# A fused attention, SiLU block and top-1 expert kernel: two weight slices change homes, the last routing goes behind the first expert tiles, and tile facts, staging and padding are re-timed

## Chip, cores and metric

The kernel runs on one core of a Trainium2 chip. The metric is the device time of one execution in microseconds; the kernel before has a median of 801.7 us over three runs (801.68 to 804.72).

Engines are named as in the profile: PE is TensorE, PEld its weight loads, ACT is ScalarE, DVE is VectorE, POOL is GpSimd, SP is SyncE, which here issues nearly all DMAs in one queue.

## What is computed

Three stages, each on the output of the one before; cut from the reference:

```
# 1. gated linear attention: 4 batches x 8 heads, 768 steps, head size 48
state = alpha[:, :, t, :, None] * state + einsum('bhd,bhe->bhde', k[:, :, t], v[:, :, t])
y[:, :, t] = einsum('bhd,bhde->bhe', q[:, :, t], state)
# 2. dense block on x = y as (3072 tokens, 384): 384 -> 2048 -> 384
h = x @ w_in;  g = h * (1.0 / (1.0 + exp(-h)));  x = g @ w_out
# 3. one expert of 8 for each token: 384 -> 1024 -> 384
logits = normalized(x) @ normalized(expert_emb).T / tau
expert_idx = argmax(logits, axis=1);  probs = softmax(logits)
out[mask] = gate_w[mask, None] * (relu(x[mask] @ w1[e]) @ w2[e])
```

## The kernel before

Numbers are kept as pairs of 16-bit halves (names with h and l, high and low part), and each product is three matmuls: high x high, high x low, low x high.

**Attention** works on 24 chunks of 128 tokens (names `S`, `yp`, `KT`, `ys`); its steps are mixed into the dense stage and end about 460 us into the span.

**The dense block** runs in 8 blocks of 384 tokens, 0 to 7, with 16 pieces of 128 hidden units (`f`). For each piece `mm1` forms `hp` in PSUM (9 matmuls, L1059), ACT makes `g` by SiLU and its high half (L1066, L1067), DVE the low half (L1068), and `mm2` adds 9 matmuls (L1082) into the three sums `o0` to `o2`. Pieces take turns on three buffers: two lie in the tile of `w2l` slice 7, the third is `g3` (shown as `g`). The input `x` of a block lies in three turns in tiles of w2's last two slices, which are only filled when the blocks no longer need them.

**Routing.** `route` takes the sums of 128 tokens after a block: square norm on ACT (L1105), logits, arg max, a rank by a small matmul (L1120, L1121), all on DVE, and scatters the row to its expert's region of the buffer `xs_d` in memory (L1149, POOL). The last block's three tiles are routed among the first expert tiles.

**Weights of the experts** (`w1`: 3 slices, `w2`: 8 slices, in 384 or 512 KB loads) are loaded by SP into a staging area `work` of 3072 words a partition, then converted to halves by ACT and DVE (L650, L651; for some L548, L551 on ACT and L552 on POOL). `begin_w` starts loads, `convert_w` converts the oldest, once per piece of blocks 6 and 7. In block 6 two loads are in flight, in block 7 three.

**Experts.** `early` (block 7) and `tile_list` (after the last routing) make a list of 28 tiles: 24 of one expert, 4 of two halves. For each tile `prep_load` loads the transposed rows `xT` and the facts `mt` (token number, scale, logits) on SP; `expert1` multiplies by `w1` in two halves of 9 matmuls (L1394) into one of two PSUM buffers, ACT takes the relu (L1400), DVE the low half (L1401); `send` transposes by DMA on SP (L1369) into `hT` (buffers `g`, `hb`, `work`); `expert2` multiplies by `w2` in 24 matmuls (L1422); ACT scales the result into `ob` (L1430, one buffer) and POOL scatters it to the output (L1433). `prep_fac` turns the logits of a tile into its gate weight: an Exp on ACT (L1359), which needs another function table than SiLU, and three small DVE operations. Before, it is called two tiles ahead, and its place on ACT is left to the scheduler. `write_pads` (L1313) copies 128 dummy rows behind each expert's last row, all eight at once on POOL after `tile_list`.

**Order.** A scheduler that builds the program places instructions on each in-order engine from its own estimate of times; where the code calls `behind(ins, other)`, an instruction is kept behind another one on the same engine. `lead["a"]` and `lead["g"]` are the latest SiLU or relu pieces on ACT and DVE, `lead["o"]` (new) the latest output scatter.

## Time and profile before

| quantity | value |
|---|---|
| median of three runs | 801.7 us |
| profiled execution, own time | 807.86 us |
| its span, first to last instruction | 806.3 us |
| busy share of the span: PE, DVE, ACT, POOL | 94%, 62%, 52%, 28% |
| mean granted PE clock | 0.981 |
| DMA queue of SP, share of 16 engines | 50.0% |

The profiled execution took 6.2 us more than the median run. The span splits into attention with blocks 0 to 5 (to about 464 us), block 6 (to 514), block 7 (to about 570), the first expert tiles, and the other tiles to about 800 us.

### The profile page before, as it was taken

What the parts mean: (1) busy time and instruction counts of PE and PEld (TensorE: products, weight loads), DVE (VectorE), ACT (ScalarE), POOL (GpSimd) and SP (SyncE); (2) the same over time, 40 slices, a digit from 0 to 9 for tenths busy, and PEclk for the clock granted to TensorE, in tenths of its full rate; (3) what the DMA queues carried; (4) which work ended last, traced back from release to release, by engine and by line L of the source; (5) the groups of instructions that cost most, each with busy time, mean ns of one, the idle gap of its engine ahead of it and who ended that gap; (6) DMA issues with size and microseconds to landing.
All of it is one profiled execution on the core that took longest, in us unless ns stands there. A gap on an engine that the chain in (4) does not pass through costs nothing. (4 is left out here: it accounts for less than half of the span.)

```text
span 806.3 us, 16490 instructions
## 1 busy us (share of the span) xinstructions
PE 756.6 (94%) x5554; PEld 472.5 (59%) x5554; DVE 498.0 (62%) x1446; ACT 418.5 (52%) x933; POOL 221.8 (28%) x322
## 2 busy tenths in 40 slices
PE   7888999999988999999999998979799999999995
PEld 4755787676655666656666654545344455555553
DVE  6599866787677977978868586665743222222221
ACT  3454655565655866857657685656632222222221
POOL 3301113554443453544232130220233011010101
PEclk9898999999999999999999999999999999999999
DMA  9599323444356445635521455255687656676562
GB/s 195 133 285 278 58 56 60 93 87 82 86 120 109 97 111 125 129 96 113 108 78 41 100 178 165 84 143 160 178 161 171 125 118 114 119 127 109 121 102 44
DMA packets 241099, 97.93 MB, mean 121 GB/s; under 512 B 222041, under 2 KB 230398, under 8 KB 240880
## 3 DMA queue, kind: packets, MB, share of 16 engines
q1 hardware_dynamic: 237424, 85.58, 50.0%
q0 software_dynamic: 3584, 11.18, 4.1%
q8 instruction: 51, 0.84, 0.5%
q14 instruction: 40, 0.33, 0.1%
HBM read 58.39 MB, written 12.16 MB: 88 GB/s over the span
## 5 line engine op out<-in xcount | busy, mean ns | idle before, releaser
L1059 PE MATMUL hp<-w2h,wi_h 128*128 128x384 f16 x576 | 145.2, 330 | 9.6 <-ACT w2l L1066 3.4
L1082 PE MATMUL o<-wo_h,w2l 128*128 128x392 f16 x528 | 146.8, 331 | 2.5 <-ACT w2l L1067 2.0
L1059 PEld LDWEIGHTS <-wi_h 128*128 128x128 f16 x768 | 74.8, 99 | 58.1 <-issue 10.6
L1082 PEld LDWEIGHTS <-w2l 128*128 128x128 f16 x792 | 75.5, 98 | 52.8 <-ACT w2l L1067 3.1
L1394 PE MATMUL hp<-w1h,xT 128*128 (+1 forms) x384 | 101.0, 382 | 4.4 <-DVE work L1401 4.3
L1401 DVE SCALAR_TENSOR_TENSOR work<-hp,work 128x512 f16<-128x512 f32 x56 | 38.5, 690 | 96.6 <-ACT work L1400 96.4
L1059 PE MATMUL hp<-w2h,wi_l 128*128 128x384 f16 x288 | 94.6, 331 | 0.0
L1082 PE MATMUL o<-wo_l,w2l 128*128 128x392 f16 x264 | 87.2, 330 | 0.0
L1394 PEld LDWEIGHTS <-xT 128*128 128x128 f16 (+1 forms) x576 | 50.4, 101 | 61.5 <-issue 7.9
L1433 POOL DMA_INDIRECT out_dram<-ob,mt x28 | 27.5, 981 | 168.4 <-ACT ob L1430 166.7
L1082 PE MATMUL o<-wo_h,g 128*128 128x392 f16 x240 | 65.8, 329 | 1.9 <-ACT g L1067 1.6
L1394 PE MATMUL hp<-w1l,xT 128*128 (+1 forms) x192 | 64.2, 382 | 0.0
L1400 ACT ACTIVATE work<-hp 128x512 f16<-128x512 f32 x56 | 33.2, 595 | 57.8 <-PE hp L1394 53.9
L1068 DVE SCALAR_TENSOR_TENSOR w2l<-w2l 128x384 f16<-128x384 f32 x88 | 50.0, 572 | 21.1 <-ACT w2l L1067 20.6
L1066 ACT ACTIVATE w2l<-hp 128x384 f32<-128x384 f32 x88 | 42.5, 484 | 32.2 <-PE hp L1059 28.7
L1059 PEld LDWEIGHTS <-wi_l 128*128 128x128 f16 x384 | 38.2, 99 | 23.7 <-issue 1.5
L1082 PEld LDWEIGHTS <-g 128*128 128x128 f16 x360 | 34.2, 98 | 25.6 <-ACT g L1067 2.3
L1059 PE MATMUL hp<-w2l,wi_h 128*128 128x384 f16 x192 | 48.7, 330 | 0.0
L1067 ACT ACTIVATE w2l<-w2l 128x384 f16<-128x384 f32 x88 | 45.4, 522 | 4.4 <-PE o L1082 2.8
L1422 PEld LDWEIGHTS <-work 128*128 128x128 f16 (+1 forms) x384 | 33.5, 101 | 22.7 <-issue 0.4
L825 POOL TENSOR_SCALAR_AFFINE_SELECT S<-S 128x512 f32<-128x512 f32 x48 | 31.4, 677 | 55.0 <-ACT S L824 54.8
L1422 PE MATMUL po<-w2h,work 128*128 (+1 forms) x256 | 43.8, 326 | 0.0
(283 smaller groups left out, 1542.1 us busy)
## 6 DMA issues: line engine op xcount, KB each, us to landing
work<-in_moe_w_dram SPq DMA_DIRECT2D x24, 512.0 KB
work<-in_moe_w_dram SPq DMA_DIRECT2D x30, 384.0 KB
w1h<-in_moe_w_in_dram SPq DMA_DIRECT2D x6, 768.0 KB
nat_a<-in_alpha_dram SPq DMA_DIRECT2D x23, 192.0 KB
nat_k<-in_k_dram SPq DMA_DIRECT2D x23, 192.0 KB
nat_q<-in_q_dram SPq DMA_DIRECT2D x23, 192.0 KB
nat_v<-in_v_dram SPq DMA_DIRECT2D x23, 192.0 KB
w1h<-in_moe_w_out_dram SPq DMA_DIRECT2D x5, 768.0 KB
```

What stands on the lines that cost most here:

```text
L825: nc.gpsimd.affine_select(out=s, in_=s, pattern=[[0, NPAIR], [1, 128]], compare_op=ALU.is_ge, fill=0.0, base=0, channel_multiplier=-1,)
L1059: ins = nc.tensor.matmul(out=hp, lhsT=wi[a][f // 2][:, c, (f % 2) * 128:(f % 2 + 1) * 128], rhs=x[:, c, :], start=(n == 0), stop=(n == 3 * ...
L1066: nc.scalar.activation(out=g, in_=hp, func=ACTF.Silu, scale=1.0 / (SX * SWI))
L1067: lead["a"] = nc.scalar.activation(out=gh, in_=g, func=ACTF.Copy, scale=SG)
L1068: lead["g"] = nc.vector.scalar_tensor_tensor(out=gl, in0=g, scalar=SG, in1=gh, op0=ALU.mult, op1=ALU.subtract)
L1082: nc.tensor.matmul(out=acc[t], lhsT=a[:, ts], rhs=wo[w][f // 2][:, f % 2, :], start=(f == 0 and n == 0), stop=(f == KF - 1 and n == 2),)
L1394: nc.tensor.matmul(out=hp[ts], lhsT=xT[:, a, ts], rhs=w1s[w][c][:, e if isinstance(e, int) else bass.ds(e, 1), fs], start=(n == 0), stop=( ...
L1400: lead["a"] = nc.scalar.activation(out=hs[:, 0], in_=hp, func=ACTF.Relu)
L1401: lead["g"] = nc.vector.scalar_tensor_tensor(out=hs[:, 1], in0=hp, scalar=0.0, in1=hs[:, 0], op0=ALU.max, op1=ALU.subtract)
L1422: nc.tensor.matmul(out=po[ts], lhsT=hT[c // 4][:, at + ts.start:at + ts.stop], rhs=w2s[w][c][:, e if isinstance(e, int) else bass.ds(e, 1) ...
L1433: nc.gpsimd.indirect_dma_start(out=out[:, :], out_offset=bass.IndirectOffsetOnAxis(ap=d["row"], axis=0), in_=ob, in_offset=None, bounds_ch ...
```

## The change

Seven edits, none of which adds or removes a matmul, a conversion, a load or a scatter:

1. Of w2's last slices, `uni` now holds `h6`, `l6`, `l5`, `l7`; the tiles of `h5` and `h7` open at pieces 13 and 15 of block 7, when memory of the dense weights comes free. Slice 5 is thus converted before the end of block 7.
2. `place` gives each load any free words of `work`, in place of fixed slots; `begin_w` allows up to four loads in flight for all but the first slices of w1 (three are asked for in blocks 6 and 7, where block 6 had two). The routing copies of blocks 5 and 6 move out of `work`.
3. The last routing is kept behind the relu of the tiles ahead of it, and its first row uses another buffer.
4. `prep_fac` is called for a tile just before its own `expert2`, behind the newest relu.
5. The list of `early` uses a buffer of its own, not `g3`.
6. `write_pads` copies two experts' pads per tile, in the turns of tiles 2 to 5, behind the output scatter ahead of them.
7. The order of the first expert tiles is written anew: tile 0's and tile 1's `expert1` come as a whole, with slice 7's conversions between.

```diff
-        for c in (KE - 2, KE - 1):
-            for s in "hl":
-                w2s[s][c] = wu.tile([128, E, DM], FP16, name=f"w2{s}{c}")
-                uni.append(w2s[s][c].rearrange("p e d -> p (e d)"))
+        for s, c in (("h", KE - 2), ("l", KE - 2), ("l", KE - 3), ("l", KE - 1)):
+            w2s[s][c] = wu.tile([128, E, DM], FP16, name=f"w2{s}{c}")
+            uni.append(w2s[s][c].rearrange("p e d -> p (e d)"))
...
+        held, newest = [], [0]
+
+        def place(n, room=3072):
+
+            for k in range(0, room, 256):
+                at = (newest[0] + k) % room
+                if at + n <= room and all(at >= b or at + n <= a for a, b in held):
+                    newest[0] = at + n
+                    held.append((at, at + n))
+                    return at
...
             def begin():
-                st = work[:, F * (e % 2):F * (e % 2 + 1)]
+                at = place(F, 2048 if c < 2 else 3072)
+                st = work[:, at:at + F]
                 ins = nc.sync.dma_start(out=st, in_=w1[e, c * 128:(c + 1) * 128, :])
...
-        def weight2(c, e, slot, pooled=False):
+        def weight2(c, e, slot=None, pooled=False):
             def begin():
-                st = slot.rearrange("p (e d) -> p e d", e=2)
+                at = place(2 * DM) if slot is None else None
+                words = work[:, at:at + 2 * DM] if slot is None else slot
+                st = words.rearrange("p (e d) -> p e d", e=2)
                 nc.sync.dma_start(out=st, in_=w2[e:e + 2, c * 128:(c + 1) * 128, :].rearrange("e p d -> p e d"))
...
             sc = 1.0 / (SG * SWO)
-            row = m2.tile([128, ROW], FP32, name="row", **(dict(tag="sq", bufs=1) if last and n != 1 else dict(tag="row", bufs=3)))
...
-                x2 = work[:, 2048 + n * DM:2048 + (n + 1) * DM] if n < 2 else m2.tile(
-                    [128, ROW], FP32, tag="sq", name="x2", bufs=1)[:, 0:DM]
+                if n == 2:
+                    x2 = m2.tile([128, ROW], FP32, tag="sq", name="x2", bufs=1)[:, 0:DM]
+                elif j + 3 < NB:
+                    x2 = work[:, 2048 + n * DM:2048 + (n + 1) * DM]
+                else:
+                    w, at = (uni[n], 6 * DM) if j + 2 == NB else (uni[1], (4 + 2 * n) * DM)
+                    x2 = w[:, at:at + 2 * DM].bitcast(FP32)
                 unit = 1.0
                 nc.scalar.activation(out=x2, in_=acc[:, 0:DM], func=ACTF.Copy, scale=sc, accum_out=fin)
-            nc.scalar.activation(out=row[:, 0:DM], in_=x2, func=ACTF.Square, scale=unit, accum_out=ss)
+            first = [nc.scalar.activation(out=row[:, 0:DM], in_=x2, func=ACTF.Square, scale=unit, accum_out=ss)]
...
-            )
+            ))
             nc.gpsimd.tensor_copy(out=meta[:, 0:1].bitcast(I32), in_=tok[:, i:i + 1])
...
-            nc.vector.tensor_reduce(out=rm, in_=x2, axis=AXX, op=ALU.max, apply_absolute_value=True)
+            first.append(nc.vector.tensor_reduce(out=rm, in_=x2, axis=AXX, op=ALU.max, apply_absolute_value=True))
+            if last:
+                for ins, order in zip(first, (lead["a"], lead["g"], lead["g"])):
+                    behind(ins, order)
...
-                weight2(c, e, work[:, 512 * (e % 4):512 * (e % 4) + 2 * DM]) + (1,) for c in range(2) for e in range(0, E, 2)
+                weight2(c, e) + (1,) for c in range(2) for e in range(0, E, 2)
             )
 
...
-                if c == KE - 1 and e < 4:
-                    st = uni[2 + i][:, 4 * DM:].bitcast(FP32)
-                else:
-                    if c == KE - 1:
-                        i = 5 - i
-                    st = work[:, 2 * DM * i:2 * DM * (i + 1)]
+                st = None
+                if c == KE - 1:
+                    i = 5 - e // 2
+                    st = work[:, 2 * DM * i:2 * DM * (i + 1)] if e > 2 else (
+                        g3 if e else uni[3][:, 4 * DM:]).bitcast(FP32)
                 todo.append(weight2(c, e, st, (c, e) in POOLW2) + (2,))
 
-        def open_w2(c):
+        def open_w2(c, parts="hl"):
             pool = wst.enter_context(tc.tile_pool(name=f"w2{c}", bufs=1, side="left", **rel))
-            for s in "hl":
+            for s in parts:
                 w2s[s][c] = pool.tile([128, E, DM], FP16, name=f"w2{s}{c}")
 
         def begin_w(k):
-            while todo and len(late) < min(k, 3 if todo[0][2] == 2 else 2):
+            while todo and len(late) < min(k, 2 if todo[0][2] == 0 and todo[0][1] < 2 else 4):
                 begin, c, kind = todo.pop(0)
                 late.append((begin(), c, kind))
...
             return tl, tcum
 
-        def listing(tl, tcum, base, n, rows, experts):
+        def listing(tl, tcum, base, n, rows, experts, gt):
...
-            gt = g3[:, 1024:].bitcast(FP32)
             G = gt[:, 0:E * n].rearrange("p (j e) -> p j e", e=E)
...
+            gt = m2.tile([128, ROW], FP32, tag="sq", name="gt", bufs=1)
+            listing(tl, tcum, base, KEARLY, idx0, ei0, gt)
             nc.vector.tensor_sub(out=es, in0=tl, in1=tcum)
...
-            listing(tl, tcum, base, NLIST, idx[:, 0:NLIST], ei)
+            listing(tl, tcum, base, NLIST, idx[:, 0:NLIST], ei, g3[:, 1024:].bitcast(FP32))
...
-        def write_pads():
-            for e in range(E):
+        def write_pads(experts):
+            for e in experts:
                 r = nc.values_load(
                     ends[0:1, e:e + 1], engines=[mybir.EngineType.Pool], min_val=0, max_val=DUMMY - 128,
                     skip_runtime_bounds_check_because="an expert has at most NT rows and CAP is NT + 128",
                 )
...
-        def prep_fac(j):
+        def prep_fac(j, order=None):
             d = tl_[j]
             meta = d.pop("m")
             s = m2.tile([128, 2], FP32, tag="s", name="s", bufs=4)
             sm, fac = s[:, 0:1], s[:, 1:2]
             ex = m2.tile([128, E], FP32, tag="ex", name="ex")
-            nc.scalar.activation(out=ex, in_=meta[:, 2:2 + E], func=ACTF.Exp, accum_out=sm)
+            ins = nc.scalar.activation(out=ex, in_=meta[:, 2:2 + E], func=ACTF.Exp, accum_out=sm)
+            if order is not None:
+                behind(ins, order)
...
-            nc.gpsimd.indirect_dma_start(
+            lead["o"] = nc.gpsimd.indirect_dma_start(
...
                     convert_w(last)
+                    if last and f >= KF - 4:
+                        begin_w(3)
+                        convert_w(last)
                 if j > 1 and (f % 4 == 2 or done[0] >= NCH):
-                    begin_w(1 if done[0] < NCH else 2 if j + 1 < NB else 3)
+                    begin_w(1 if done[0] < NCH else 3)
                 mm2(j, f, g, acc)
                 g = nxt
                 if last:
                     if f % 2:
                         fpool[f // 2].close()
-                    if f % 4 == 3:
+                    if f % 4 == 3 and f + 1 < KF:
                         open_w2(2 + f // 4)
+                    elif f == KF - 3:
+                        open_w2(KE - 3, "h")
+                    elif f == KF - 1:
+                        open_w2(KE - 1, "h")
...
-        while todo and todo[0][1] == 5:
-            late.append((todo.pop(0)[0](), 5, 2))
-        for _ in range(2):
-            late.append((todo.pop(0)[0](), KE - 1, 2))
+        begin_w(4)
+        while late[0][1] == KE - 3:
+            convert_w()
+            begin_w(4)
+        expert1(0, 0, True)
         convert_w()
         convert_w()
-        expert1(0, 0)
-        convert_w()
-        convert_w()
-        for _ in range(2):
-            late.append((todo.pop(0)[0](), KE - 1, 2))
+        send(0, 0)
         expert1(0, 1)
         convert_w()
         convert_w()
-        expert1(1, 0, True)
-        convert_w()
-        convert_w()
-        send(1, 0)
+        expert1(1, 0)
         expert1(1, 1)
         assert not todo and not late
-        prep_fac(0)
-        prep_fac(1)
...
         expert2(1, 0)
+        prep_fac(0, lead["a"])
         expert2(0, 1)
         send(2, 0)
         send(2, 1)
         prep_load(3)
         prep_load(4)
-        prep_fac(2)
-        prep_fac(3)
         expert1(3, 0, True)
         expert1(3, 1, True)
+        prep_fac(1, lead["a"])
         expert2(1, 1)
         send(3, 0)
         send(3, 1)
         tile_list()
-        write_pads()
         order = [*range(SFULL), *range(NFULL, NFULL + SPAIR)]
         for n in range(2, len(order)):
             j = order[n]
+            if n < 6:
+                write_pads(range(2 * n - 4, 2 * n - 2))
             if n + 3 < len(order):
                 prep_load(order[n + 3])
-            if n + 2 < len(order):
-                prep_fac(order[n + 2])
             if 2 < n and n + 1 < len(order):
                 expert1(order[n + 1], 0)
...
+            prep_fac(j, lead["a"])
             expert2(j)
 
```

The build's order shows the first differences on PE, ACT and DVE at the end of block 5; on SP a load moves ahead of one transpose shortly before. Line numbers of the change are 16 to 25 higher.

First place: ACT in block 7, at pieces 5 to 9. `ex,s<-mt` is the Exp of `prep_fac`, L650 a conversion of w2, L1066 and L1067 the SiLU pieces. Before:

```order
L1067 ACTIVATE g_179<-g_179 128x384
L1066 ACTIVATE g_179<-hp 128x384
L1359 ACT_TABLE_LOAD
L1359 ACTIVATE ex,s<-mt 128x8
L1067 ACTIVATE w2l_178<-w2l_178 128x384
L650 ACTIVATE w2h_6959<-work 128x768
L1359 ACTIVATE ex,s<-mt 128x8
L1067 ACTIVATE w2l_178<-w2l_178 128x384
L650 ACTIVATE w2h_6959<-work 128x768 x2
L1067 ACTIVATE g_179<-g_179 128x384
L650 ACTIVATE w2h_6959<-work 128x768
L1359 ACTIVATE ex,s<-mt 128x8 x2
```

Now, over pieces 5 to 9 (L1082 and L1083 are the SiLU pieces, L649 the conversion):

```order
L1082 ACTIVATE g_179<-hp 128x384
L1083 ACTIVATE g_179<-g_179 128x384
L649 ACTIVATE w2h_6960<-work 128x768
L1082 ACTIVATE w2l_178<-hp 128x384
L1083 ACTIVATE w2l_178<-w2l_178 128x384
L649 ACTIVATE w2h_6960<-work 128x768
L1082 ACTIVATE w2l_178<-hp 128x384
L1083 ACTIVATE w2l_178<-w2l_178 128x384
L649 ACTIVATE w2h_6960<-work 128x768
L1082 ACTIVATE g_179<-hp 128x384
L1083 ACTIVATE g_179<-g_179 128x384
L649 ACTIVATE w2h_6960<-work 128x768
```

The four Exps and both table loads have left this place; each piece is followed by one conversion.

Second place: ACT where block 7 ends. L1105 is the first step of the last routing, L1400 the relu of an expert tile. Before:

```order
L551 ACTIVATE w2h_7173<-work 128x768
L1105 ACTIVATE row,nx<-o_6790 128x384
L650 ACTIVATE w2h_7269<-work 128x768 x2
L1105 ACTIVATE row,nx<-o_6791 128x384
L1400 ACTIVATE work<-hp_7285 128x512
L650 ACTIVATE w2h_7269<-work 128x768 x2
L1400 ACTIVATE work<-hp_7304 128x512
L650 ACTIVATE w2h_177<-w2h_177 128x768
L650 ACTIVATE w2h_177<-w2l_178 128x768
L1135 ACTIVATE row<-o_6790,nx 128x384
L1400 ACTIVATE work<-hp_7324 128x512
L650 ACTIVATE w2h_177<-work 128x768 x2
```

Now (L1126 routing, L1425 relu, L649 conversion; `w2h_7238` is slice 5, `w2h_7286` slice 7):

```order
L1083 ACTIVATE w2l_178<-w2l_178 128x384
L649 ACTIVATE w2h_7238<-work 128x768 x4
L1425 ACTIVATE work<-hp_7295 128x512
L649 ACTIVATE w2h_7286<-w2l_178 128x768
L649 ACTIVATE w2h_7286<-g_179 128x768
L1425 ACTIVATE work<-hp_7312 128x512
L649 ACTIVATE w2h_7286<-work 128x768 x2
L1425 ACTIVATE work<-hp_7332 128x512
L1425 ACTIVATE work<-hp_7345 128x512
L1126 ACTIVATE row,nx<-o_6791 128x384
L1126 ACTIVATE row,nx<-o_6792 128x384
```

The routing steps moved from ahead of the first relu to behind the fourth, and four conversions of slice 5, which stood behind the routing, stand ahead of everything.

Third place: POOL after the last routing. L1313 is a pad, L1309 the register load that it needs, L1433 an output scatter. Before:

```order
L1433 DMA out_dram<-ob,mt 3072x384
L1309 TENSOR_LOAD ends
L1313 ISA
L1313 DMA xs_d<-xs_d 16x3152
L1433 DMA out_dram<-ob,mt 3072x384
L1309 TENSOR_LOAD ends
L1313 ISA
L1313 DMA xs_d<-xs_d 16x3152
L1309 TENSOR_LOAD ends
L1313 ISA
```

Now (L1335 pad, L1331 register load, L1458 output scatter):

```order
L1458 DMA out_dram<-ob,mt 3072x384
L1331 TENSOR_LOAD ends
L1335 ISA
L1335 DMA xs_d<-xs_d 16x3152
L1331 TENSOR_LOAD ends
L1335 ISA
L1335 DMA xs_d<-xs_d 16x3152
L1458 DMA out_dram<-ob,mt 3072x384
L1331 TENSOR_LOAD ends
L1335 ISA
L1335 DMA xs_d<-xs_d 16x3152
L1331 TENSOR_LOAD ends
```

Eight pads in a row behind two scatters have become pairs with a scatter between them.

## Rows read from the trace of the kernel before

**Rows 1.** Windows: start:end, length, busy us (x instructions) PE, PEld, DVE, ACT, POOL, PEclk, DMA share, GB/s.

```profile
464.00:514.00 50.00, 47.92 (x295) 27.81 (x294) 32.16 (x110) 31.24 (x61) 7.54 (x12) 1.00 0.50 154
514.00:570.00 56.00, 49.51 (x298) 27.97 (x297) 35.42 (x129) 38.18 (x78) 12.77 (x14) 1.00 0.53 156
570.00:602.00 32.00, 26.56 (x140) 13.40 (x139) 21.28 (x93) 13.76 (x27) 8.33 (x12) 0.95 0.73 150
602.00:640.00 38.00, 35.37 (x185) 17.85 (x183) 11.31 (x42) 11.72 (x34) 10.16 (x14) 1.00 0.68 151
640.00:800.00 160.00, 156.88 (x1017) 85.02 (x1014) 37.51 (x98) 42.39 (x117) 20.45 (x21) 1.00 0.60 110
```

**Rows 2.** Waits of PE, 464 to 800 us: releaser, us in total, times, longest.

```profile
PE hp L1394 <- DVE work L1401: 4.3, 2, 4.1
PE hp L1059 <- ACT w2l L1066: 3.4, 3, 1.7
...
PE o L1082 <- ACT w2l L1067: 2.0, 3, 0.8
PE o L1082 <- ACT g L1067: 1.6, 1, 1.6
PE hp L1059 <- ACT g L1066: 1.5, 1, 1.5
```

**Rows 3.** Timeline of ACT, blocks 6 and 7: start, us, instruction [idle before <- releaser].

```profile
486.58 0.84 ACT L650 ACTIVATE w2h<-work 128x768 f16<-128x768 f32 x1 [2.06 <-DMA work<-in_moe_w_dram]
488.82 0.84 ACT L650 ACTIVATE w2h<-work 128x768 f16<-128x768 f32 x1 [1.40 <-DMA work<-in_moe_w_dram]
...
531.37 0.52 ACT L1067 ACTIVATE g<-g 128x384 f16<-128x384 f32 x1 [2.73 <-DVE g L1266]
...
534.87 1.28 ACT L1359 ACT_TABLE_LOAD   x1
538.59 0.21 ACT L1359 ACTIVATE ex<-mt 128x8 f32<-128x8 f32 x1 [2.44 <-DMA mt<-xs_d]
...
547.09 1.28 ACT L1066 ACT_TABLE_LOAD   x1
548.39 0.49 ACT L1066 ACTIVATE w2l<-hp 128x384 f32<-128x384 f32 x1
```

**Rows 4.** Timeline of ACT where block 7 ends.

```profile
570.00 1.56 ACT L650 ACTIVATE w2h<-work 128x768 f16<-128x768 f32 x2
...
572.19 0.60 ACT L1400 ACTIVATE work<-hp 128x512 f16<-128x512 f32 x1 [0.16 <-DVE w2l L651]
```

**Rows 5.** Timelines of DVE (first two rows) and PE, the same stretch.

```profile
572.41 0.93 DVE L651 SCALAR_TENSOR_TENSOR w2l<-work,w2h 128x768 f16<-128x768 f32 x1
574.07 0.68 DVE L1401 SCALAR_TENSOR_TENSOR work<-hp,work 128x512 f16<-128x512 f32 x1
...
574.80 1.01 PE L1394 MATMUL hp<-w1h,xT 128*128 x2 [4.07 <-DVE work L1401]
578.04 0.81 PE L1422 MATMUL po<-w2h,g 128*128 x4
...
580.05 0.59 PE L1394 MATMUL hp<-w1h,xT 128*128 x2
...
581.99 0.49 PE L1422 MATMUL po<-w2h,hb 128*128 x2
```

**Rows 6.** Timelines of SP's queue and PE in the tile loop: the second half's transpose, and its first use.

```profile
630.26 1.31 SPq L1369 DMA_TRANSPOSE hb<-work  x1
634.08 0.81 PE L1422 MATMUL po<-w2h,hb 128*128 x4 [1.20 <-DMA hb<-work]
...
691.73 1.25 SPq L1369 DMA_TRANSPOSE hb<-work  x1
696.53 0.81 PE L1422 MATMUL po<-w2h,hb 128*128 x4
```

**Rows 7.** DMA issues, 560 to 640 us: issue, KB each, median us to landing.

```profile
xs_d<-xs_d POOLq DMA_DIRECT2D x8, 197.0 KB, 2.9
```

More of the change, by code (lines that the diff above doesn't have):

```diff
@@ L667, in convert @@
                 def convert():
+                    held.pop(0)
                     split_after(st, SW1, w1s["h"][c][:, e, :], w1s["l"][c][:, e, :])
@@ L1092, in route @@
             sc = 1.0 / (SG * SWO)
-            row = m2.tile([128, ROW], FP32, name="row", **(dict(tag="sq", bufs=1) if last and n != 1 else dict(tag="row", bufs=3)))
+            row = m2.tile([128, ROW], FP32, name="row", **(dict(tag="sq", bufs=1) if last and n == 0 else dict(tag="row", bufs=3)))
             meta, x16 = row[:, DM:], row[:, 0:DM].bitcast(FP16)
@@ L1277, in early @@
             nc.vector.tensor_scalar(out=base, in0=iota8, scalar1=float(CAP), scalar2=None, op0=ALU.mult)
-            listing(tl, tcum, base, KEARLY, idx0, ei0)
+            gt = m2.tile([128, ROW], FP32, tag="sq", name="gt", bufs=1)
+            listing(tl, tcum, base, KEARLY, idx0, ei0, gt)
             nc.vector.tensor_sub(out=es, in0=tl, in1=tcum)
@@ L1313, in write_pads @@
                 ins = nc.gpsimd.dma_start(out=xs_d[bass.ds(r, 128), :], in_=xs_d[DUMMY:DUMMY + 128, :])
+                behind(ins, lead["o"])
                 for other in scattered[-TPB:] + early_loads + pads:
```

5 lines of the change are left out of this document (3 added, 2 removed).

## The prediction

> **What bounds the kernel now.** I read the summary first: PE is busy for 94% of the span, no other engine for more than 62%. So the time is PE's work plus PE's idle time, and an edit is worth only the PE idle time that it removes. I then cut the span into stretches. In the windows [rows 1] the reader is to see how little room there is. In the loop of expert tiles, 640 to 800 us, PE is busy for 156.88 of 160 us, and the gaps left are scattered. Before 464 us the orders of the two kernels read the same, except for one load of w1 that SP issues ahead of a transpose; I take that stretch as unchanged. Four stretches are left. Block 6 idles 50 - 47.92 = 2.1 us, block 7 56 - 49.51 = 6.5, the start of the expert tiles 32 - 26.56 = 5.4, and the next tiles 38 - 35.37 = 2.6. That is 16.6 us in all, and it caps the gain but for one thing: the granted clock of the third stretch is 0.95.
>
> Next I asked PE's waits who ends these gaps [rows 2], and the timelines why that engine was late. In block 6 it is ACT's SiLU, 1.5 us, and just ahead of it ACT stood in conversions whose load had not landed, 2.06 and 1.40 us [rows 3]. In block 7 it is ACT again: 1.6 us for the high half in `g`, 3.4 for SiLU into `w2l`, and 2.0 for its high half there, of which 0.5 must lie in block 6 to fill its 2.1. ACT's timeline gives two causes. One SiLU half waits 2.73 us for DVE's list at L1266, which shares `g3` with it, at 531.37 us. And the Exps of `prep_fac` stand in the queue ahead of SiLU pieces: they wait for `mt` (2.44 us for the first) and need two table loads of 1.28 us each [rows 3].
>
> At the start of the expert tiles, ACT runs a routing step (the order in the change's second place shows it) and two conversions before the first relu [rows 4], DVE a low half L651 and only then L1401, and PE waits 4.07 us for it. After that wait its matmuls are slow: nine from 574.80 to 578.04 us, 3.24 us, where nine from 580.05 to 581.99 take 1.94 [rows 5]. That is 1.3 us more than the idle time counts.
>
> **The change part by part.** All terms are microseconds of PE.
>
> *Block 6, deeper staging.* The loads that ACT waited for start one conversion earlier. With two in flight ACT got one every 2.24 us there, from 486.58 to 488.82 [rows 3], and a third should cover a late one. Of the 1.5 us wait I leave 0.5. Gain 1.0, bounds -1.5 (more loads beside the blocks' own make another piece as late) and 1.5.
>
> *Block 7, list and Exps.* The list's own buffer removes its tie to `g3`: 1.6 us, and up to 1.7 of the two L1066 waits just before it (3.4 less the longest), in which DVE is busy with routing and list. The Exps leave block 7, so the table loads (2.56 us of ACT), the `mt` waits and what they made late go: the longest L1066 wait, 1.7, stands behind the second table load, and the two L1067 waits in `w2l`, 2.0 - 0.5, behind Exps, 3.2 in all [rows 2]. Each piece then has on ACT two SiLU steps of about 0.5 and one conversion of 0.84 [rows 3], 1.9 us, against 18 matmuls on PE: nine at 1.94 and nine a little shorter (widths 512 and 384), over 3 us. So ACT has slack, and I leave 0.8 of 6.5. Gain 5.7, bounds 3.2 (the Exps' part alone, with the list's waits coming back as waits for conversions) and 6.5. The Exps' new place costs nothing by itself: one table load remains, after the last SiLU, and an Exp of 0.21 stands behind a relu with about a tile, 24 matmuls at 0.163 and 18 at 0.216 us or 7.8 us [rows 5], until its gate weight is needed by `ob`. If that cover fails, `ob` frees its sum late, and PE waits in each tile.
>
> The Trainium skill, in "ScalarE: Activation LUTs", What ACT_TABLE_LOAD costs, puts a switch at 1283 ns and another 1380 ns of drain. The load agrees with the 1.28 us of this trace; the drain does not, since the next ACTIVATE starts at 548.39, 0.02 us after 547.09 + 1.28 [rows 3]. By the page two switches dropped would free 5.3 us of ACT and not 2.6; the sum above goes by PE's waits and would stay.
>
> *Start of the expert tiles.* I follow the new chain from the moment when block 7's sums are complete (0). The tile of h7 opens then. ACT: conversions to 0.8 and 1.6 (1.56 for two [rows 4]), relu of tile 0's second half to 2.2 (0.60 [rows 4]). DVE: two L651 of 0.93 to 2.8, L1401 of 0.68 to 3.5 [rows 5]. PE has ten matmuls of tiles 0 and 1 by then, 2.2, and waits 1.3. The nine of tile 1's second half end at 5.4. Tile 0's first transpose leaves when the conversion out of `g3` is through, at 2.8, and needs 3.8 from issue to use, as 630.26 to 634.08 [rows 6]: 6.6, a wait of 1.2. Then the 24 matmuls of `expert2` (twelve and two tiny ones from 578.04 to 580.05 [rows 5]) with 18 of `expert1` between them take 7.8, to 14.4. The first of tile 2's halves ends at 10.5 on the way; its relu, low half and transpose (0.6, 0.7, 3.8) end at 15.6, a wait of 1.2. Together 3.7 of idle time, in pieces of 1.3 at most, against 5.4 + 1.3 slow = 6.7. I assume that pieces this short don't slow the matmuls; the one of 4.07 did. Gain 3.0. Bounds: 6.7 with all hidden; -3 if slice 5's or slice 7's loads land late (rival A). The routing, now behind four relus, costs nothing as long as its list is ready before its tiles; DVE has 21.28 busy us of 32 here [rows 1].
>
> *Tiles to 640 us.* The idle 2.6 holds a wait of 1.2 for `hb` [rows 6]. Its transpose needed 3.82 us to its use there, and another, at 691.73, was used after 4.80 us without a wait: a margin of about 1.0 [rows 6]. Eight pads of 197 KB in a row, each 2.9 us to landing [rows 7], become pairs over four tiles. I leave 1.5. Gain 1.1, bounds -2 (half a microsecond in each of four tiles) and 2.6.
>
> The Trainium skill, in "DMA: Bandwidth & Descriptors", Issuing engines are not separate DMA queues, says that DMAs from any engine interleave on the same 16 DMA engines. Nothing in these rows speaks against it: the DMA share is 0.73 and 0.68 where the pads run, 0.60 after [rows 1]. By it, pads on POOL's queue delay SP's transposes in four tiles instead of in one burst: rival B.
>
> *Sum.* 1.0 + 5.7 + 3.0 + 1.1 = 10.8. The profiled execution took 807.86 us, so 797.1 in the same terms; against the median of 801.7, 790.9. I say **791.0 us**. The ends of all bounds add up to -3.3 and 17.3.
>
> **The rivals.** *A: the loads of slices 5 and 7 come late.* Five loads of slices 5 and 7 are begun around block 7's last pieces, and at 2.24 us each [rows 3] the last lands 11 us after the first. Then the first conversions stand as routing did, and the start keeps its stall: the third term goes from 3.0 to between 0 (all the 6.7 as before) and -3 (of those 11 us some 8 lie behind block 7's own pieces or the first transposes, and 3 don't; an estimate). Total 4.8 to 7.8, 794 to 797 us. For it: ACT's waits for loads in block 6 [rows 3]. Against: the staging area is freed piece by piece, so the loads need not start together.
>
> *B: little remains.* The pads beside the transposes eat more than the margin of 1.0 in four tiles, or the pieces of block 7 find another wait (DVE's low half, 35.42 busy us of 56 [rows 1]) behind ACT's. Terms two and four shrink to 3 and -2, with the others small: 0 to 4, about 799.5. For it: the DMA shares above. Against: PE's waits in block 7 name ACT alone.
>
> *C: slower.* The chain of one tile on SP, facts, first transpose, `xT`, second transpose, has the margin of 1.0 us. If the Exp just ahead of `ob` makes the scatter, and with it the next tile's scaled result and its transposes, 1.6 us later per tile, PE waits 0.6 in each of 24 tiles, 14.4, and the net is 4 lost: about 806. It decides from 10.8 / 24 = 0.45 us a tile. Against it: the steady loop hides all but 3.1 of 160 us, and Exp is 0.21 us behind a relu that ACT ran anyway.
>
> *D: more than forecast.* The start hides all its waits, and the blocks too: over 14 gained, about 786.
>
> **How the numbers follow.** Forecast, 8 to 14 gained, 787.7 to 793.7: 0.60. D 0.05, A 0.17, B 0.13, C 0.05. A change of 0.5% is 4 us, 797.7 and 805.7; less than that is about what a measurement of this kernel can tell from no change. Faster by more: 0.60 + 0.05 + 0.17 = 0.82. Within: 0.13, slower: 0.05. The range of 786 to 798 holds the forecast, A, and most of D; the 0.18 of B and C lie outside.
>
> **What would show it.** Right: no table load and no Exp between the last routing of block 6 and the end of block 7; L1067's successor never waits for DVE's list; PE's idle time in block 7 under 2 us; a PE wait of under 2 at the first relu's low half, and no fall of the granted clock behind it. In tiles 2 to 6, waits for `hb` and `g` of 1.2 at most, and past 640 us PE as busy as now. Wrong: conversions of slice 5 or 7 that wait for a load and PE behind them (A); waits for `hb` in each tile with pads (B); a wait of PE for ACT's `ob` once per tile (C). An idle time in block 7 that stays above 4 would fell my reading of the Exps.

## The result, and the profile after

The changed kernel takes 792.6 us in the median (four runs, 789.8 to 796.6) against 801.8 before; the ratio is 0.9881 with a 95% interval of 0.9840 to 0.9921, so 9 us or 1.2% faster. The forecast was 791.0 us, in a range of 786 to 798. In a later set of runs the same two kernels had a ratio of 0.9863 (0.9839 to 0.9887).

The profiled execution took 792.25 us, 15.6 less than that of before (807.86). Some of this is not the change. Here are the windows of the stretch ahead of block 6, first of the kernel before, then of the changed one, then of a kernel of the experiments (edits 4 and 5 alone) whose program is that of before in this stretch (columns as in [rows 1]):

```profile
0.00:460.00 460.00, 436.38 (x3604) 298.06 (x3605) 357.49 (x973) 278.87 (x616) 162.57 (x249) 0.97 0.52 115
```

```profile
0.00:456.00 456.00, 430.44 (x3602) 294.48 (x3603) 357.18 (x972) 278.00 (x615) 164.15 (x249) 0.99 0.52 117
```

```profile
0.00:456.00 456.00, 433.16 (x3605) 296.19 (x3606) 356.66 (x973) 278.81 (x616) 165.39 (x249) 0.99 0.53 116
```

Block 6 begins at 460.1, 456.5 and 456.0 us. The first and the third run the same program up to there and still differ by 4.1 us, with granted clocks of 0.97 and 0.99. So 3.6 us of the difference between the two profiles is spread between executions, and 12.0 is left behind it.

The windows of the changed kernel, cut at its own places: block 6, block 7, start of the tiles to tile 4, tiles 4 to 8, tiles 8 to 24:

```profile
456.00:503.00 47.00, 47.00 (x292) 27.96 (x291) 33.51 (x109) 32.48 (x63) 7.69 (x12) 1.00 0.58 175
503.00:557.00 54.00, 54.00 (x330) 31.48 (x328) 37.91 (x127) 37.97 (x73) 13.19 (x14) 1.00 0.54 157
557.00:599.00 42.00, 36.08 (x194) 18.46 (x193) 25.14 (x116) 17.06 (x41) 13.34 (x20) 1.00 0.68 155
599.00:631.00 32.00, 32.00 (x175) 16.92 (x173) 7.29 (x20) 8.79 (x26) 5.60 (x7) 1.00 0.67 142
631.00:758.00 127.00, 126.04 (x715) 66.10 (x714) 29.15 (x80) 32.87 (x98) 15.66 (x16) 1.00 0.61 114
```

PE is busy for the whole of blocks 6 and 7, where it idled 2.1 and 6.5 us [rows 1], and for the whole of tiles 4 to 8. Nearly all that is left stands at the start of the tiles. PE's waits from 456 us to 790 (the one for `bad` belongs to the kernel's end):

```profile
PE hp L1419 <- DVE work L1426: 3.1, 2, 2.4
PE pb L1607 <- DVE bad L1471: 1.9, 1, 1.9
PE hp L1419 <- issue: 1.3, 4, 0.4
PE po L1447 <- DMA g<-work: 1.2, 2, 0.6
PE po L1447 <- DMA work<-work: 1.0, 1, 1.0
PE po L1447 <- DMA hb<-work: 0.9, 1, 0.9
PE hp L1419 <- DVE mx L1133: 0.2, 1, 0.2
```

The SiLU waits of [rows 2] (L1066, L1067 there) are gone; the wait for the relu's low half is 2.4 in place of 4.1.

For the experiments I use one measure of each profile, taken from the start times of PE's matmuls: the time of a stretch, less its matmuls at the length that they have undisturbed in the trace (0.1625 us for `mm1`, 0.1656 `mm2`, 0.2155 `expert1`, 0.1631 `expert2`). It counts waits and slow clock together. "Start" is from block 7's last `mm2` to tile 4's `expert2`; tiles 4 to 8 are given in full (31.1 is 4 undisturbed tiles of 7.78), tiles 8 to 24 as the time over 16 x 7.78 us. Ratios are to the kernel before, on the chip of the run.

| kernel | block 6 | block 7 | start | tiles 4-8 | tiles 8-24 | ratio (95%) |
|---|---|---|---|---|---|---|
| before | 2.9 | 7.7 | 9.0 | 33.2 | 0.7 | 1 |
| changed | 0.3 | 0.2 | 7.2 | 31.1 | 2.5 | 0.988 (0.984-0.992) |
| changed, again | 0.3 | 0.2 | 7.4 | 31.1 | 5.1 | 0.986 (0.984-0.989) |
| edit 4 undone | 0.3 | 5.5 | 8.4 | 38.0 | 2.0 | 0.9995 (0.997-1.002) |
| edit 4 undone in the loop | 0.3 | 0.2 | 6.5 | 38.8 | 1.6 | 0.991 (0.988-0.995) |
| edit 5 undone | 0.3 | 6.1 | 8.0 | 31.4 | 4.0 | 0.993 (0.991-0.996) |
| before with edits 4 and 5 | 3.2 | 1.0 | 8.1 | 33.5 | 4.1 | 0.996 (0.994-0.998) |
| two loads in block 6 | 0.3 | 0.2 | 7.0 | 31.1 | 2.9 | 0.987 (0.984-0.990) |
| two loads, fewer words | 4.2 | 0.2 | 7.9 | 31.3 | 3.0 | 0.989 (0.987-0.992) |
| routing copies back | 2.8 | 1.2 | 10.4 | 31.7 | 2.1 | 0.990 (0.987-0.992) |
| pads at once | 0.3 | 0.2 | 11.1 | 31.1 | 2.3 | 0.992 (0.989-0.995) |
| routing ahead of relus | 0.3 | 0.2 | 7.7 | 31.1 | 2.4 | 0.987 (0.985-0.990) |
| words rotated | 0.3 | 0.2 | 6.5 | 31.1 | 4.7 | 0.986 (0.983-0.990) |
| constant expert | 0.3 | 0.2 | 11.7 | 31.1 | 2.2 | 0.986 (0.983-0.989) |

The change in the two profiles is thus 2.6 in block 6, 7.5 in block 7, 1.9 at the start and 2.1 in tiles 4 to 8, less 1.9 in tiles 8 to 24.

### The profile page after: what moved, and what is told of

Same layout as the page of the kernel before. It is cut to its first block, busy times and chain, and to the rows that moved or that the text cites. A ratio compares the mean times of both kernels' runs of the same rounds, so it can differ in the third digit from the quotient of the medians.

```text
span 790.6 us, 16507 instructions
## 1 busy us (share of the span) xinstructions
PE 748.7 (95%) x5554; PEld 469.7 (59%) x5554; DVE 496.2 (63%) x1446; ACT 413.0 (52%) x931; POOL 223.5 (28%) x322
## 5 line engine op out<-in xcount | busy, mean ns | idle before, releaser
L1075 PE MATMUL hp<-w2l,wi_h 128*128 128x384 f16 x480 | 120.3, 326 | 0.0
L1075 PE MATMUL hp<-w2l,wi_l 128*128 128x384 f16 x240 | 78.2, 326 | 0.0
L1458 POOL DMA_INDIRECT out_dram<-ob,mt x28 | 27.8, 993 | 168.4 <-ACT ob L1455 158.8
L1075 PE MATMUL hp<-w2h,wi_h 128*128 128x384 f16 x288 | 70.6, 326 | 2.4 <-DMA w2h<-ys 1.2
L1425 ACT ACTIVATE work<-hp 128x512 f16<-128x512 f32 x56 | 33.4, 597 | 73.1 <-PE hp L1419 62.9
L1084 DVE SCALAR_TENSOR_TENSOR w2l<-w2l 128x384 f16<-128x384 f32 x88 | 51.8, 591 | 24.5 <-ACT w2l L1083 24.2
L1455 ACT ACTIVATE ob<-po,s 128x384 f32<-128x384 f32 x28 | 16.3, 581 | 86.1 <-PE po L1447 78.6
L1082 ACT ACTIVATE w2l<-hp 128x384 f32<-128x384 f32 x88 | 42.6, 484 | 31.8 <-PE hp L1075 28.4
L1083 ACT ACTIVATE w2l<-w2l 128x384 f16<-128x384 f32 x88 | 45.6, 522 | 4.5 <-PE o L1098 3.0
L1447 PEld LDWEIGHTS <-work 128*128 128x128 f16 (+1 forms) x384 | 33.5, 101 | 23.6 <-DMA work<-work 1.5
```

The lines of the kernel that those rows point to most:

```text
L1075: ins = nc.tensor.matmul(out=hp, lhsT=wi[a][f // 2][:, c, (f % 2) * 128:(f % 2 + 1) * 128], rhs=x[:, c, :], start=(n == 0), stop=(n == 3 * ...
L1082: nc.scalar.activation(out=g, in_=hp, func=ACTF.Silu, scale=1.0 / (SX * SWI))
L1083: lead["a"] = nc.scalar.activation(out=gh, in_=g, func=ACTF.Copy, scale=SG)
L1084: lead["g"] = nc.vector.scalar_tensor_tensor(out=gl, in0=g, scalar=SG, in1=gh, op0=ALU.mult, op1=ALU.subtract)
L1425: lead["a"] = nc.scalar.activation(out=hs[:, 0], in_=hp, func=ACTF.Relu)
L1447: nc.tensor.matmul(out=po[ts], lhsT=hT[c // 4][:, at + ts.start:at + ts.stop], rhs=w2s[w][c][:, e if isinstance(e, int) else bass.ds(e, 1) ...
```

## The experiments

**Edit 4 undone.** The gate weight two tiles ahead, as in the kernel before.

```diff
         assert not todo and not late
+        prep_fac(0)
+        prep_fac(1)
         prep_load(2)
...
-            prep_fac(j, lead["a"])
+            if n + 2 < len(order):
+                prep_fac(order[n + 2])
```

> The changed kernel with edit 4 undone: the gate weight of a tile is made two tiles ahead again. In the order the first four Exps stand in block 7 again, this time with two pairs of table loads there (four of 1.28 us) where the kernel before had one pair. Measure in the profile: the stretch from block 7's first matmul of mm1 to tile 4's first matmul of expert2, 105.95 us before and 96.56 us after the change, with the same PE work in it. My theory, that the Exps and what they wait for cost 3.2 us of PE's waits: the stretch is 99.5 to 102.5 us and the median 3 to 6 us above the changed kernel's 792.6. Rival, that the list's own buffer alone gave block 7 its time and the Exps only filled ACT's idle time: the stretch stays within 1 us of 96.6 and the median within 2 us of 792.6.

Block 7 lost 5.3 us again: the direction of the theory, but more than its 3.2, and the stretch of 103.0 us lies above its 99.5 to 102.5. The ratio is 0.9995: the whole gain was gone, not 3 to 6 us of it. Tiles 4 to 8 took 38.0 us, which neither theory nor rival had. Rows of this kernel's ACT timeline, in block 7 and in the tiles:

```profile
529.78 1.28 ACT L1382 ACT_TABLE_LOAD   x1
533.65 0.21 ACT L1382 ACTIVATE ex<-mt 128x8 f32<-128x8 f32 x1 [2.59 <-DMA mt<-xs_d]
...
536.47 1.28 ACT L1082 ACT_TABLE_LOAD   x1
537.76 0.49 ACT L1082 ACTIVATE w2l<-hp 128x384 f32<-128x384 f32 x1
...
613.29 0.21 ACT L1382 ACTIVATE ex<-mt 128x8 f32<-128x8 f32 x1 [5.89 <-DMA mt<-xs_d]
613.40 0.19 ACT L1382 ACTIVATION_READ_ACCUMULATOR ex<-mt 128x1 f32 x1
613.49 0.56 ACT L1455 ACTIVATE ob<-po,s 128x384 f32<-128x384 f32 x1
613.96 0.19 ACT L1455 ACTIVATION_READ_ACCUMULATOR ob<-po,s 128x1 f32 x1
614.05 1.17 ACT L1425 ACTIVATE work<-hp 128x512 f16<-128x512 f32 x2
...
625.40 0.21 ACT L1382 ACTIVATE ex<-mt 128x8 f32<-128x8 f32 x1 [10.18 <-DMA mt<-xs_d]
```

In the tiles the Exp waits 5.9 and 10.2 us for the facts of a tile two ahead. Behind it stand `ob` and the relus of two halves, which run the moment that it is through. PE then waits for transposes, longest for `hb`, 2.68 us at 627 us:

```profile
605.29 0.81 PE L1447 MATMUL po<-w2h,g 128*128 x4 [1.39 <-DMA g<-work]
...
608.42 0.81 PE L1447 MATMUL po<-w2h,hb 128*128 x4 [1.02 <-DMA hb<-work]
...
627.00 0.81 PE L1447 MATMUL po<-w2h,hb 128*128 x4 [2.68 <-DMA hb<-work]
```

For this longest wait the relus are not what was late. DVE had made their low halves by 616.0 us (1.29 us from 614.67), but SP issued the transpose only at 621.99, behind a load of `xT` in its queue. The waits of SP's queue from 610 to 632 us, and its two rows:

```profile
SPq L1367 <- DMA out_dram<-ob,mt: 6.6, 2, 3.4
SPq L1366 <- DMA xs_d<-xs_d: 2.2, 1, 2.2
```

```profile
620.02 1.24 SPq L1366 DMA_TRANSPOSE xT<-xs_d  x1
...
621.99 1.25 SPq L1394 DMA_TRANSPOSE hb<-work  x1
```

The load of facts (L1367) waits for an output scatter, which needs `ob`, which stands on ACT behind the Exp; the load of `xT` waits for a pad, which edit 6 keeps behind a scatter. So the Exp's wait goes round by the scatter and SP's queue and comes back as late facts and late transposes.

**Edit 4 undone in the loop alone.** Is that a consequence of the stall in block 7, or of the Exp's place in the loop? Tiles 0 and 1 as in the changed kernel, tiles 2 and later two ahead.

```diff
+        prep_fac(2)
+        prep_fac(3)
         expert1(3, 0, True)
...
+            if n + 2 < len(order):
+                prep_fac(order[n + 2])
...
-            prep_fac(j, lead["a"])
             expert2(j)
```

> The changed kernel with edit 4 undone in the loop of the tiles alone: tiles 0 and 1 get their gate weights late, tiles 2 and later two tiles ahead, as before. No Exp returns to block 7. Theory from the run with all of edit 4 undone, where ACT stood 3 to 10 us in an Exp that waits for its facts, with ob and the next relu queued behind it: the stretch from tile 4 to tile 8 rises from 31.14 to 35 to 38 us, block 7 and the start stay within 1 us of 96.56, and the median lies 4 to 7 us above the changed kernel. Rival, that the long waits there came from the stall in block 7 that pushed everything on: the stretch stays within 1 us of 31.1.

Blocks 6 and 7 stay as changed, and tiles 4 to 8 take 38.8 us. The rival falls: the place in the loop does it by itself. The theory was short here too (35 to 38 us), while the ratio of 0.991 against 0.986 to 0.988 is 2 to 4 us, under its 4 to 7. The same queue on ACT:

```profile
616.34 0.21 ACT L1382 ACTIVATE ex<-mt 128x8 f32<-128x8 f32 x1 [6.67 <-DMA mt<-xs_d]
...
616.55 0.56 ACT L1455 ACTIVATE ob<-po,s 128x384 f32<-128x384 f32 x1
617.01 0.19 ACT L1455 ACTIVATION_READ_ACCUMULATOR ob<-po,s 128x1 f32 x1
617.11 1.07 ACT L1425 ACTIVATE work<-hp 128x512 f16<-128x512 f32 x2
```

**Edit 5 undone.**

```diff
-            gt = m2.tile([128, ROW], FP32, tag="sq", name="gt", bufs=1)
-            listing(tl, tcum, base, KEARLY, idx0, ei0, gt)
+            listing(tl, tcum, base, KEARLY, idx0, ei0, g3[:, 1024:].bitcast(FP32))
```

> The changed kernel with edit 5 undone: the early list is made in g3 again. My theory: the SiLU piece in g waits for the list, and the same stretch (block 7's first matmul to tile 4's expert2, 96.56 us) gets 1.6 to 3.3 us longer, 98.2 to 99.9; the median rises by as much, to about 795. Rival, that with the Exps gone ACT and DVE have enough slack to hide the list: the stretch stays within 0.7 of 96.6.

The stretch named there took 103.3 us: the theory's direction, but past its 99.9. Block 7 lost 5.8 us, of which two waits of 0.6 and one of 2.4 for SiLU are seen directly. ACT's timeline there shows the tie: the high half in `g` waits for the list.

```profile
523.26 0.52 ACT L1083 ACTIVATE g<-g 128x384 f16<-128x384 f32 x1 [3.54 <-DVE g L1287]
```

PE's clock then fell: 0.50 for 3.4 us from 524.8, which costs about 1.7 of the 5.8.

```profile
524.80:528.20 3.40, 3.40 (x13) 1.57 (x11) 1.28 (x3) 1.24 (x3) 0.00 (x0) 0.50 0.15 30
```

**Edits 4 and 5 alone,** on the kernel before (their lines as in the diff of the change):

```diff
+            gt = m2.tile([128, ROW], FP32, tag="sq", name="gt", bufs=1)
+            listing(tl, tcum, base, KEARLY, idx0, ei0, gt)
...
+            prep_fac(j, lead["a"])
             expert2(j)
```

> The kernel before with edits 4 and 5 alone: gate weights just before their tile's expert2, and the early list in a buffer of its own. Undone one by one in the changed kernel, edit 4 gave 6.4 us back up to tile 4 and 6.8 from tile 4 to 8, edit 5 gave 6.7 up to tile 4: more than the whole change saved there, so that they are no sum. My theory, that these two carry most of the change: the stretch from block 7's first matmul to tile 4's expert2 falls from 105.95 to 99 to 101, the one to tile 8 from 33.2 to 31 to 32, and the median lies 6 to 9 us below the kernel before. Rival, that each edit only pays once all the others are there: less than 4 us in all.

Block 7 falls from 7.7 to 1.0: the two carry it. Undone one at a time they gave back 5.3 and 5.8, together more than the 7.5 that there was. With all other edits in place, block 7 keeps 5.5 of its 7.7 where edit 4 alone is missing (with two pairs of table loads for one) and 6.1 where edit 5 is; so each by itself saves little there and both together nearly all. Block 6 and tiles 4 to 8 stay as before (33.5 us, against the theory's 31 to 32), the start within 0.9; the stretch up to tile 4 is 98.3, under the theory's 99 to 101. The ratio of 0.996 is 3 us: the theory said 6 to 9, and the rival, under 4, has the total. The gain in block 7 is there, but tiles 8 to 24 took 4.1 us over their matmuls in this profile, 3.4 more than before. All stretches of the table together give 3.7, near the 3 us of the nine runs, so that loss may be more than one execution's chance.

**Block 6, in three runs.** First two loads in flight instead of three:

```diff
-                    begin_w(1 if done[0] < NCH else 3)
+                    begin_w(1 if done[0] < NCH else 2 if j + 1 < NB else 3)
```

> The changed kernel with two loads in flight in block 6 instead of three; all else stays. Measure: block 6 from its first matmul to block 7's first, 48.67 us before and 46.09 after. My theory, that the depth of the staging is what took the conversions' waits away: the stretch is 47.5 to 48.7 us, the median 1.5 to 2.6 us above 792.6. Rival, that the free words and the moved routing copies did it and not the depth: it stays at 46.1 to 46.5.

Nothing changed: the depth, to which the prediction gave its first term, is worth nothing in this kernel. Then the same with 2048 words for these loads instead of 3072:

```diff
-                at = place(F, 2048 if c < 2 else 3072)
+                at = place(F, 2048)
...
-                at = place(2 * DM) if slot is None else None
+                at = place(2 * DM, 2048 if c < 2 else 3072) if slot is None else None
```

> The changed kernel with two loads in flight in block 6 and with the words for the last slice of w1 and the first two of w2 limited to 2048, as before; the routing copies stay out of the staging area. The depth alone gave nothing. Block 6 took 48.67 us before and 46.09 after the change. Theory: the third place in the staging area took the conversions' waits away, since with two places a load must wait for both halves of the conversion before the last; block 6 returns to 47.5 to 48.7 us. Rival, that the routing copies that lay in the staging area held it: block 6 stays at 46.1 to 46.6.

And three loads and all words, but the routing copies of blocks 5 and 6 in the staging area again. Loads and copies share words here, so that the routing works on other values; the amount of work in block 6 is the same.

```diff
-                elif j + 3 < NB:
+                else:
                     x2 = work[:, 2048 + n * DM:2048 + (n + 1) * DM]
-                else:
-                    w, at = (uni[n], 6 * DM) if j + 2 == NB else (uni[1], (4 + 2 * n) * DM)
-                    x2 = w[:, at:at + 2 * DM].bitcast(FP32)
```

> The changed kernel with the routing copies of blocks 5 and 6 back in the staging area, and everything else as changed. Theory as in the run with fewer words: the places count and not the copies alone, so block 6 stays within 0.8 us of 46.09. Rival: the copies hold the words that the loads want, and block 6 rises to 47.5 or more; block 7's first pieces, 0.2 us over their matmuls after the change, then wait too.

Both bring block 6 back: 50.0 and 48.6 us for 46.1. The words are the cause, and the copies had to leave so that the loads could have them; my theory for the last run, that the copies alone don't matter, falls. The 50.0 us, above the theory's 48.7, are one wait of 2.18 us and a fall of the clock behind it (last section). ACT's conversions of `w2` wait for loads 9.0 us in block 6 in the kernel before (first fence), 8.9 with fewer words (second), 3.3 in the changed kernel (third):

```profile
ACT w2h L650 <- DMA work<-in_moe_w_dram: 9.0, 8, 2.1
```

```profile
ACT w2h L649 <- DMA work<-in_moe_w_dram: 8.9, 7, 2.2
```

```profile
ACT w2h L649 <- DMA work<-in_moe_w_dram: 3.3, 4, 1.6
```

**Edit 6 undone.**

```diff
         tile_list()
+        write_pads(range(E))
...
-            if n < 6:
-                write_pads(range(2 * n - 4, 2 * n - 2))
...
-                behind(ins, lead["o"])
```

> The changed kernel with edit 6 undone: all eight pads in a row after the last list. Measures in the profile: from tile 4's first matmul of expert2 to tile 8's, 33.21 us before and 31.14 after, and from tile 8's to tile 24's, 125.13 and 127.00. My theory, that the burst of pads makes transposes late: the first stretch gets 1 to 2 us longer, the second stays, and the median rises by 1 to 2. Rival 1, that the pairs of pads beside the transposes are what costs the later tiles their 1.9 us: the second stretch falls to 125 to 126. Rival 2, that pads have nothing to do with either: both stay within 0.5 us.

Tiles 4 to 8 don't move: the pads had no part in the 2.1 us there. But the pads run ahead of tile 4, and the start is 11.1 us, by a wait of 2.80 for a transpose and two falls of the clock. This profile alone can't put that down to the pads, since the kernel with the constant expert number (below), whose program is that of the changed kernel up to tile 8, has 11.7 with a like wait. The two rows, first with the pads at once:

```profile
594.91 1.42 PE L1446 MATMUL po<-w2h,work 128*128 x4 [2.80 <-DMA work<-work]
```

```profile
597.04 0.81 PE L1447 MATMUL po<-w2h,work 128*128 x4 [2.02 <-DMA work<-work]
```

The times of all runs say more. On the same chip the profiled execution with the constant number was the slowest of five by 5.5 us (799.25; the others 791.5 to 793.8), while with the pads at once all four took 795.1 to 799.7. The ratio of 0.992 (0.989 to 0.995) lies above the 0.986 to 0.988 of the six kernels in the table whose other stretches are those of the changed one, though their intervals touch. So edit 6 seems to be worth some 4 us, more than the 1 to 2 of my theory and not where I looked for it. How the pads would do it isn't shown.

**The order of edit 3 undone.**

```diff
-            if last:
-                for ins, order in zip(first, (lead["a"], lead["g"], lead["g"])):
-                    behind(ins, order)
```

> The changed kernel with the order of edit 3 undone: the last routing's first steps are no longer kept behind the relus; its other buffer stays. In the order a routing step stands ahead of the first relu on ACT again. Measure: PE's time over its matmuls (each at its length at full clock) from block 7's last matmul to tile 4's expert2: 9.0 us before, 7.2 after. My theory, that routing ahead of the relus was part of the stall at the start: it rises by 1 to 2.5 us, to between 8.2 and 9.7. Rival, that the conversions of slices 5 and 7 hold the start and the routing only fills ACT's waits for them: within 0.7 us of 7.2.

7.7 against 7.2 and 7.4: the rival's range. Where the routing stands is worth half a microsecond at most. That the conversions and their loads hold the start instead is read from the rows below, for the first wait; this run doesn't show it.

**Words rotated.** The changed kernel's rows at the start (ACT, DVE, PE) show what ties the first relu:

```profile
555.12 0.84 ACT L649 ACTIVATE w2h<-work 128x768 f16<-128x768 f32 x1 [1.25 <-DMA work<-in_moe_w_dram]
556.16 0.84 ACT L649 ACTIVATE w2h<-work 128x768 f16<-128x768 f32 x1 [0.19 <-DMA work<-in_moe_w_dram]
558.09 0.60 ACT L1425 ACTIVATE work<-hp 128x512 f16<-128x512 f32 x1 [1.09 <-DVE w2l L650]
```

```profile
557.03 0.96 DVE L650 SCALAR_TENSOR_TENSOR w2l<-work,w2h 128x768 f16<-128x768 f32 x1
...
558.72 0.69 DVE L1426 SCALAR_TENSOR_TENSOR work<-hp,work 128x512 f16<-128x512 f32 x1 [0.72 <-ACT work L1425]
```

```profile
559.47 0.59 PE L1419 MATMUL hp<-w1h,xT 128*128 x2 [2.44 <-DVE work L1426]
...
562.21 0.59 PE L1419 MATMUL hp<-w1h,xT 128*128 x2 [0.64 <-DVE work L1426]
...
564.92 0.81 PE L1447 MATMUL po<-w2h,g 128*128 x4 [0.62 <-DMA g<-work]
```

Slice 5's last loads land late (waits of 1.25 and 0.19), DVE's half of the last conversion ends at 558.0, and the relu writes words that it read.

```diff
+                newest[0] += 2 * DM if e == 0 and c in (2, 4) else 0
                 at = place(2 * DM) if slot is None else None
```

> The changed kernel with one more edit: the staging words of slices 2 to 5 are rotated by two places, so that slice 5's last two loads lie in words that the first tile's relu doesn't write. In the order the first relu moves ahead of the last conversion of slice 5 on ACT. In the changed kernel PE waits 2.44 us for that relu's low half, and the relu 1.09 us for a low half of slice 5. My theory, that these words tie the start of the tiles to slice 5's late loads: the wait of 2.44 falls below 1.2, and the stretch from block 7's first matmul to tile 4's expert2 falls from 96.56 us by 1 to 2. Rival, that the loads themselves are late and the conversions of slices 5 and 7 then hold the first transposes: the wait moves to a transpose or to the second relu and the stretch stays within 0.5 us of 96.6.

The wait fell from 2.44 to 1.54, but the second one grew from 0.64 to 1.35, and later ones of 1.00 (for `xT`) and 1.64 came: the start is 6.5 for 7.2, and the stretch 95.8 for 96.6. That is 0.7 us, between the theory's 1 to 2 and the rival's 0.5, and the ratio is that of the changed kernel; the waits moved as the rival said.

**Constant expert number.**

```diff
-                    (ts, src if isinstance(src, int) else nc.values_load(
+                    (ts, j % E if KEARLY <= j < NFULL else src if isinstance(src, int) else nc.values_load(
```

> The changed kernel with a constant expert number in place of the one read from the list for all full tiles from tile 8 on, so that these tiles multiply by the wrong expert's weights; the work on each engine stays, only the register load of the expert number on PE ahead of each of these tiles, and the indexing by it, are gone. In the changed kernel PE waits 0.2 to 0.5 us ahead of some tiles with nothing but that load (0.3 to 0.95 us) ahead of them. My theory, that these waits are the 1.9 us that the later tiles lost: the stretch from tile 8 to tile 24 falls from 127.0 to 124.5 to 125. Rival, that the transposes or the facts come late there: it stays above 126.

The waits named "issue" are gone from tiles 8 to 24, and the stretch is still 126.7 us; a wait of 0.86 for `hb` stands there instead. My theory that the register loads are the time lost in the later tiles falls.

**The changed kernel again,** with no edit.

> The changed kernel once more, for the spread between executions of the same program. Theory: the differences that the runs so far show in the later tiles (124.5 us of matmuls from tile 8 to tile 24, and 1.5 to 4.7 us over them, whatever was undone) and from tile 1 to tile 4 (1.2 to 5.2 us over the matmuls) are such spread and not effects of the edits: this profile differs from the first by over 0.5 us in at least one of the two, while blocks 6 and 7 and the stretch from tile 4 to tile 8 agree within 0.1 us. Rival, that the program's own order sets them: all stretches agree within 0.3 us. The median is 8 to 13 us under the kernel before.

Blocks 6 and 7 and tiles 4 to 8 agree within 0.03 us, the start within 0.2, tiles 8 to 24 differ by 2.6: spread, as expected. The start's agreement hides a difference: the first wait is 3.09 for 2.44, and the clock falls behind it.

## Why the prediction was right

*The size.* 10.8 us were forecast, 9.2 measured (9 to 13 by the interval of the second set's ratio); the two profiles differ by 12.0 from block 6 on. That the sum comes so near is partly luck. In the profiles the four terms together are 14.1 and not 10.8: three are under-sized and one over-sized. Tiles 8 to 24, which the sum put at nothing, took 1.9 back there, and 4.4 in the second profile of the changed kernel.

*Block 6: the right gain by the wrong step, and under-sized* (1.0, measured 2.6). The step "a third load in flight should cover a late one" is wrong. A load waited for words: with all words two in flight give what three give, and without them block 6 is as slow as before.

*Block 7* (5.7, measured 7.5): right in its cause, under-sized. The list and the Exps are the cause, as ACT's waits behind PE's named them, and both must go. What I left over, 0.8, didn't remain, and the measure counts 7.7 there where I counted 6.5 of idle time. The term's split, about half for the list and 3.2 for the Exps, as if they added up, was wrong: either one alone, put back, costs 5.3 to 5.8. The trace also bears out the sum's use of rows for the function table: in the kernel with edit 4 undone an activation follows 0.01 us behind a table load (537.76 after 536.47 + 1.28), so here too the drain that the Trainium skill gives in "ScalarE: Activation LUTs", What ACT_TABLE_LOAD costs (1380 ns), isn't seen.

*Start* (3.0, measured 1.9): over-sized. The step that failed is "relu of tile 0's second half": the chain took tile 0's first half as done by the end of block 7. It was held up by slice 5's loads to 558.09, 1.6 us after the last `mm2` at 556.49; so the first wait was 2.44 and not 1.3. That is rival A in a small size. So one of the signs that I named, a wait under 2 there, failed. The clock's fall was avoided in this profile and not in the second one. The routing's move, which the term contained, is worth 0.5 at most. The 1.9 itself isn't clear of chance: the program of the changed kernel up to tile 8 took 7.2, 7.4 and once, in the kernel with the constant number, 11.7. No run undoes edits 1 and 7, so what they are worth here isn't shown.

*Tiles to 640 us* (1.1, measured 2.1 in tiles 4 to 8): right in sign, wrong in cause for these tiles. I gave it to the spread of the pads, and the pads do nothing in tiles 4 to 8. The term's window began at 602 us, though, where the kernel before writes its pads, and tile 4 at 614.67; what the pads do ahead of tile 4 the table counts to the start, and there edit 6 seems to pay. In the changed kernel the Exp's place in the loop is necessary (38.8 us without it), but not sufficient: with edits 4 and 5 alone the stretch is 33.5. What else it needs, among the homes of the slices and the new order at the start, wasn't tried.

*Rival C* had the sign of the Exp's move in the loop wrong: just ahead of `ob` it waits for nothing, two tiles ahead it held `ob` and two relus for 6 us. A small part of C may still be true. Over 16 x 7.78 us, the three kernels with the Exp two tiles ahead in the loop take 0.7, 2.0 and 1.6 in tiles 8 to 24, the eleven others 2.1 to 5.1, 3.2 in the mean. That would be 1.8 us lost to edit 4 there, against 7.6 gained in tiles 4 to 8. The three are the lowest of the fourteen, but with a spread of 2.6 between two executions of one program it isn't shown, and the version that would use both places wasn't run. No kernel here is clearly faster than the changed one.

## What to carry to other kernels

An instruction whose result is only needed later belongs behind the work that is due now, not early in the queue: on an in-order engine its wait for a transfer is a wait of all that stands behind it. A deeper prefetch is worth what the free space lets it be; count the places that the loads can land in before the loads in flight. Undo edits one by one and also make them alone: here two edits, each worth over 5 us in block 7 when undone, were worth 6.8 there together. And before a stretch of one profile is called the effect of an edit, or not its effect, look at the times of all runs.

## What the runs showed of the hardware that was not expected

PE's granted clock fell behind some waits of PE and not behind others of like length. Windows of 6 us behind the wait of 2.44 us in the changed kernel, of 3.09 in its second run, and of 2.18 in block 6 with fewer words. In all three PE had shown no other wait for 46 us or more ahead of it:

```profile
560.00:566.00 6.00, 4.75 (x24) 2.13 (x22) 5.37 (x13) 4.53 (x10) 0.69 (x2) 1.00 0.52 95
```

```profile
560.00:566.00 6.00, 4.98 (x16) 1.95 (x16) 5.50 (x11) 4.25 (x7) 0.00 (x0) 0.72 0.37 77
```

```profile
488.00:494.00 6.00, 5.72 (x25) 3.03 (x25) 3.97 (x11) 3.71 (x8) 0.00 (x0) 0.72 0.58 168
```

The column before the last two is the clock: 1.00, 0.72 and 0.72, the second and third with a piece at the lower of the two levels (1.2 GHz). The wait of 2.44 didn't bring it, the one of 2.18 did:

```profile
488.28 0.48 PE L1075 MATMUL hp<-w2h,wi_h 128*128 128x384 f16 x2 [2.18 <-ACT g L1082]
```

Other waits fit no order of length either: 2.02 and 2.08 us had a fall behind them, 2.75 and 2.82 in other kernels had none. So a stall's price has two parts, its length and in some executions a slow stretch behind it, and the second makes two profiles of one program differ.
